# Pooled attention and a mixture of four attention experts: the order table's units divided at each change of engine, and the table arranged anew

## The chip, the cores and the metric

The kernel runs on one core of a Trainium2 chip. The metric is the device time of one execution in microseconds (us), median of the runs shown; less is better.

## What is computed

Eight batches, each with 8 heads, 576 rows and head size 64. First an attention whose keys and values are averaged in groups of 8 rows (72 pooled rows), then four causal attention experts over the joined heads (512 wide), of which the two with the highest gate logits are added per row:

```python
k_p = k.reshape(B, H, Sp, pool, D).mean(axis=3)      # pool = 8
v_p = v.reshape(B, H, Sp, pool, D).mean(axis=3)
attn = softmax(q @ k_p.T / sqrt(D))                  # 576 x 72 for each head
x = join_heads(attn @ v_p)                           # (B, 576, 512)
logits = x @ w_gate                                  # 4 experts
w = softmax of the two largest logits, 0 for the others
for e in range(4):
    a = softmax(causal((x @ wq[e]) @ (x @ wk[e]).T / sqrt(Hd)))
    out += w[..., e] * (a @ (x @ wv[e]) @ wo[e])
```

## The kernel before

The work of a batch is cut into **units**, small functions that each issue a few instructions on several engines. Rows 0 to 511 of a batch are its main part; the last 64 rows of two batches are taken together as one tail block of 128 rows (units of the odd batch). The units, with their lines in the kernel before:

- Loads (SyncE's DMA queue, SP): `lq`, `lk`, `lv` (main rows, 1 MB each; for batch 0 in two halves `lqa`, `lqb` and so on), `lqt`, `lkt`, `lvt` (the tails), `W:lq`, `W:lk`, `W:lv`, `W:lo` (weights; `W:lv` brings the small gate weights too).
- Preparation: `ks`, `vs` add neighbouring rows of k and v, `qc` casts q to bf16, `kt`, `vt`, `qt` cast the tails. From batch 1 on they run on GpSimd (POOL); for batch 0 they are spread over VectorE (DVE), ScalarE (ACT) and POOL.
- First attention: `kp` and `vp` pool k and v by matmuls; `q0` to `q3` transpose q; `s0` to `s3` make scores (matmuls that use 64 rows of the array) and their exponentials on ACT; `a0` to `a3` multiply by v and scale on DVE; `x0` to `x3` transpose the result.
- Experts: `v0`, `v2` make values and gate logits, `p0` to `p3` the projections (evacuated by ACT), `g1` to `g6` the gates (DVE, POOL, ACT and POOL, DVE, POOL), `c00`, `c01`, `c10`, `c11`, `c2` the causal scores (64-row matmuls, exponentials on ACT, masks on POOL), `o0`, `o1` the product with the values and its scaling on DVE, `t0`, `t1` transposes, and `w`, `y`, `z` units the product with `wo`, its evacuation by ACT or DVE and the store.
- Tail block: `qx`, `sx`, `ax`, `xx`, `pt`, `vx`, `h0`, `h1`, `hd`, `ox`, `tx`, `w4` in the same sense.

`in_order` keeps every instruction in the program's order on its own engine, so a program order is also each engine's queue. That order is written out by hand as the table `ORDER` of 501 unit names at the top; the last lines of the kernel run through it and call each unit once. A unit issues all its instructions at its place. If unit A stands ahead of unit B, then A's instructions are ahead of B's on PE, on DVE, on ACT, on POOL and on SP alike. For example `scores` of part A (unit `s`) issues two matmuls and the exponential together:

```python
            ps = ps2.tile([128, 2, MAIN], FP32, name="sA_ps", tag="ps2")
            ...
            et = etp.tile([SP, 2, MAIN], BF16, name="etA", tag="etA")
            act.activation(out=et[:], in_=ps[0:SP, :, :], func=EXP, scale=ATT_EXP_SCALE)
```

Matmul results go to two pools of PSUM buffers: `ps1` (2 buffers of one bank: `kp`, `vp`, `q`, `x`, `p`, `t`, `w`, `y` and the tail block's `qx`, `xx`, `pt`, `vx`, `ox`, `tx`, `w4`) and `ps2` (3 buffers of two banks: `s`, `a`, `v`, `c`, `o`, `z`, `sx`, `ax`, `h`, `hd`). A PE group waits until the engine that evacuates the buffer's previous content is through. Raw inputs have two buffers each, the tail of q one, output tiles four (`ofin`). All DMAs are issued by SP, in the table's order, and a store that waits for its copy holds back the loads behind it.

Of the kernel before, what the change touches and what calls it, by code (L numbers as in the profile page):

```python
# [53 lines left out]
def kernel(  # L54
# [126 lines left out]
    units = {}  # L181
# [49 lines left out]
    pairs = {}  # L231

    def part_a(b: int):
# [55 lines left out]
        def pool_k(p0, p1):  # L289
            ps = ps1.tile([128, NHP, SP], FP32, name="kpT_ps", tag="ps1")  # L290
            for hp in range(p0, p1):
# [9 lines left out]
                )  # L301
            dve.tensor_copy(out=kp[:, p0:p1, 0:SP], in_=ps[:, p0:p1, :])

        def pool_v():
# [5 lines left out]
            for half in range(2):  # L310
# [3 lines left out]
                )  # L314
            dve.tensor_copy(
# [3 lines left out]
        def q_t(hp):  # L319
# [3 lines left out]
            for r in range(NR):  # L323
# [3 lines left out]
                )  # L327
            dve.tensor_copy(
# [3 lines left out]
        def scores(hp):  # L332
            ps = ps2.tile([128, 2, MAIN], FP32, name="sA_ps", tag="ps2")
            for hh in range(2):
# [4 lines left out]
                )  # L339
            et = etp.tile([SP, 2, MAIN], BF16, name="etA", tag="etA")  # L340
# [3 lines left out]
        def av(hp):  # L344
# [4 lines left out]
            for hh in range(2):  # L349
                h = 2 * hp + hh  # L350
                for c in range(NTC):
# [4 lines left out]
                    )  # L356
            view = ps[:, :, 0 : NTC * (D + 1)].rearrange("p e (c d) -> p e c d", c=NTC)
# [11 lines left out]
        def x_t(fc):  # L369
            ps = ps1.tile([128, MAIN], BF16, name="xT_ps", tag="ps1")  # L370
            for c in range(NTC):
# [3 lines left out]
                )  # L375
            dve.tensor_copy(out=xT[:, fc, :], in_=ps[:])
# [32 lines left out]
    def part_p(b: int):  # L409
# [5 lines left out]
        def proj(j):  # L415
            ps = ps1.tile([128, MAIN], FP32, name="p_ps", tag="ps1")
            for fc in range(NFC):
# [3 lines left out]
                )  # L421
            act.copy(out=qk[:, j, :], in_=ps[:])
# [6 lines left out]
        def values(c0):  # L429
            L = logits()  # L430
            ps = ps2.tile([128, 2, 512], FP32, name="v_ps", tag="ps2")
            for cl in range(2):
                c = c0 + cl
                for fc in range(NFC):
# [3 lines left out]
                    )  # L438
            dve.tensor_copy(out=L[:, c0 : c0 + 2, :], in_=ps[:, :, E * HD : NVG])
# [84 lines left out]
    def part_s(b: int):  # L524
# [19 lines left out]
        def scores(ep, i):  # L544
            if ep not in st["et"]:
# [311 lines left out]
```

## Time and profile before

| | us |
|---|---|
| runs | 180.79, 181.35, 184.5 |
| median | 181.35 |
| span of the profiled execution (its own time) | 180.5 |
| PE busy | 157.6 |
| DVE busy | 131.6 |
| ACT busy | 121.4 |
| POOL busy | 105.0 |

The profile page and the trace belong to one execution, whose time is its span from the first to the last instruction. PE is TensorE, PEld its weight loads. A PE row's end is modelled: a matmul's record lasts longer than the time until the next may start, so the start-to-start time of two groups tells more than their durations. In a timeline row stand the start, the duration, the engine, the operation, output and inputs, the shape, the count, and in brackets the idle time before it with what ended it. Because every operation goes through one helper, all rows bear the helper's line L100, and groups are known by their tiles.

### The profile page before, as it was taken

To read this page: it belongs to the slowest core of one execution; us is meant where nothing else is said; L and a number is where in the kernel's file an instruction comes from. 1 tells how busy PE (TensorE), PEld (TensorE's weight loads), DVE (VectorE), ACT (ScalarE), POOL (GpSimd) and SP (SyncE) were. 2 spreads that over 40 slices of the span, in tenths; PEclk is the share of its full clock that TensorE was granted. 3 is DMA by queue.
4 is the path that set the end of the run, shared out by engine and by line. 5 is a ranking of instruction groups with operands and counts; after the bars stand their busy time and mean duration, and the time that the engine had idled before them with its cause. 6 is when DMAs were issued, how large, how long until landed. Compare 5 with 4: busy or idle time off the path is not lost.

```text
span 180.5 us, 5221 instructions
## 1 busy us (share of the span) xinstructions
PE 157.6 (87%) x2080; PEld 100.5 (56%) x2080; DVE 131.6 (73%) x363; ACT 121.4 (67%) x165; POOL 105.0 (58%) x212
## 2 busy tenths in 40 slices
PE   0046977799999999999999999999999999999970
PEld 0022465357766756765675667666666674665530
DVE  0166786589799787898877886977687877787850
ACT  2022600778497976887898688888788887778821
POOL 8953357437989879578988577726301253453200
PEclk9999999999999999999999999999999999999997
DMA  4999999999999999999999994325130333152964
GB/s 141 311 300 183 328 347 202 232 310 329 182 349 317 329 232 318 292 266 313 272 334 302 367 349 142 91 60 189 47 117 3 100 136 122 58 165 78 337 236 123
DMA packets 50200, 40.19 MB, mean 223 GB/s; under 512 B 20736, under 2 KB 45312, under 8 KB 50176
## 3 DMA queue, kind: packets, MB, share of 16 engines
q1 hardware_dynamic: 50176, 39.86, 79.6%
q8 instruction: 16, 0.26, 0.7%
q14 instruction: 8, 0.07, 0.1%
HBM read 30.42 MB, written 9.44 MB: 221 GB/s over the span
## 4 chain that ended last, share of the span: by engine, by line
PE 75%; SPq 13%; DMA 5%; DVE 2%; ACT 1%; issue 1%; POOL 1%; DVEq 0%; ACTq 0%; POOLq 0%
PE p_ps L100 15%; SPq L100 13%; PE y_ps L100 8%; PE v_ps L100 7%; PE sB_ps L100 6%; PE oB_ps L100 5%; DMA qtail<-in_q_dram 5%; PE xT_ps L100 4%; PE sA_ps L100 4%; PE oA_ps L100 4%; PE qT_ps L100 4%; PE oBt_ps L100 3%; PE oT_ps L100 2%; PE vp_ps L100 2%; PE pt_ps L100 2%; PE kpT_ps L100 2%
## 5 line engine op out<-in xcount | busy, mean ns | idle before, releaser
L100 ACT ACTIVATE etA<-sA_ps 72x1024 bf16<-72x1024 f32 x32 | 32.0, 1018 | 19.6 <-PE sA_ps L100 19.4
L100 ACT ACTIVATE etB<-sB_ps 128x1024 bf16<-128x1024 f32 x32 | 31.7, 1026 | 2.4 <-PE sB_ps L100 2.1
L100 PE MATMUL p_ps<-xT,wqk 128*128 128x512 bf16 x128 | 32.3, 379 | 0.0
L100 POOL TENSOR_SCALAR_AFFINE_SELECT etB<-etB 128x256 bf16<-128x256 bf16 x48 | 18.7, 407 | 14.9 <-ACT etB L100 12.4
L100 ACT CAST qk<-p_ps 128x512 bf16<-128x512 f32 x32 | 18.7, 584 | 12.3 <-PE p_ps L100 12.0
L100 DVE TENSOR_TENSOR x_tm<-oA_ps,rzA 128x512 bf16<-128x512 f32 x32 | 22.1, 692 | 1.1
L100 POOL TENSOR_TENSOR vsum<-vraw 128x512 bf16<-128x512 f32 (+1 forms) x16 | 19.0, 1210 | 3.9 <-DMA vraw<-in_v_dram 3.4
L100 PEld LDWEIGHTS <-wqk 128*128 128x128 bf16 x192 | 14.6, 97 | 10.4 <-issue 0.5
L100 POOL TENSOR_TENSOR ksum<-kraw 128x512 bf16<-128x512 f32 x14 | 17.4, 1266 | 3.4 <-DMA kraw<-in_k_dram 3.4
L100 PE MATMUL y_ps<-wo_t,oT 128*128 128x512 bf16 x64 | 18.2, 379 | 0.1
L100 PE MATMUL v_ps<-wvg,xT 128*128 128x260 bf16 x128 | 17.4, 281 | 0.1
L100 POOL CAST qbf<-qraw 128x2048 bf16<-128x2048 f32 x7 | 13.2, 1891 | 7.0 <-DMA qraw<-in_q_dram 7.0
L100 DVE COPY qT<-qT_ps 128x512 bf16<-128x512 bf16 x32 | 13.2, 419 | 4.4 <-PE qT_ps L100 3.9
L100 DVE COPY xT<-xT_ps 128x512 bf16<-128x512 bf16 x32 | 13.0, 419 | 2.9 <-PE xT_ps L100 2.6
L100 PE MATMUL qT_ps<-ident,qbf 128*128 128x128 bf16 x128 | 13.5, 235 | 1.5 <-DVE kp L100 0.7
L100 ACT COPY ofin<-y_ps 128x512 f32<-128x512 f32 x20 | 11.5, 586 | 4.8 <-ACT etB L100 1.9
L100 PE MATMUL sA_ps<-qT,kp 64*128 64x512 bf16 x64 | 12.8, 412 | 1.6 <-DVE kp L100 0.9
L100 PE MATMUL sB_ps<-qk 64*128 64x256 bf16 (+3 forms) x128 | 13.9, 300 | 0.2 <-ACT etB L100 0.2
L100 PEld LDWEIGHTS <-etA 72*128 72x128 bf16 x256 | 11.5, 101 | 4.2 <-ACT etA L100 0.7
L100 PE MATMUL oA_ps<-vp,etA 72*128 72x65 bf16 x256 | 13.6, 200 | 0.0
L100 PEld LDWEIGHTS <-xT 128*128 128x128 bf16 x128 | 12.1, 100 | 2.4 <-DVE xT L100 0.4
L100 PE MATMUL xT_ps<-perm,x_tm 128*128 128x128 bf16 x128 | 12.6, 231 | 0.8 <-DVE x_tm L100 0.7
(119 smaller groups left out, 324.0 us busy)
## 6 DMA issues: line engine op xcount, KB each, us to landing
qraw<-in_q_dram SPq DMA_DIRECT2D x7, 1024.0 KB, 9.2
kraw<-in_k_dram SPq DMA_DIRECT2D x7, 1024.0 KB, 8.3
vraw<-in_v_dram SPq DMA_DIRECT2D x7, 1024.0 KB, 10.4
out_dram<-ofin SPq DMA_DIRECT2D x28, 256.0 KB, 2.3
kraw<-in_k_dram SPq DMA_DIRECT2D x2, 512.0 KB, 4.8
ktail<-in_k_dram SPq DMA_DIRECT2D x16, 64.0 KB, 6.9
qraw<-in_q_dram SPq DMA_DIRECT2D x2, 512.0 KB, 7.3
vtail<-in_v_dram SPq DMA_DIRECT2D x16, 64.0 KB, 7.1
```

The source lines that it names most:

```text
L100: return tc.keep_in_program_order(fn(*args, **kwargs))
```

## The change

Each unit becomes a generator: where its work passes from one engine to another, a `yield` stands, and the table names the unit once for each part. The 501 names become 920 entries. The parts of a unit keep their order, and each engine's queue can now have an order of its own. The table is arranged anew over all engines; buffers, tiles and instructions stay. The tail buffer of q is made by whichever of the two batches loads first.

```diff
 ORDER = """
-0:lka 0:lkt 0:lkb 0:lqb 0:qcb1 0:lqa 0:lvt 0:ksb 0:qcb0 0:kt 0:lvb 0:qca0 0:kpb 0:lva W:lv 0:ksa
-1:lq 0:q3 0:qca1 0:vt 0:q0 0:q1 0:vsa 1:lkt 0:s3 1:lk 1:lv 0:kpa 0:lqt 0:vsb 0:vp 0:s0 1:qc 0:q2
-W:cv 0:s1 0:a0 0:s2 0:a3 0:a1 0:a2 0:x1 0:x3 1:q0 0:x2 1:lvt 0:x0 W:lq 1:q2 1:ks 0:v2 1:lqt 0:v0
-1:kt 1:q3 1:kp W:lk 0:g1 1:vs 2:lq 1:s2 1:s3 2:lkt 1:q1 W:c2 1:s1 0:g2 0:g3 1:vt 1:vp 2:lk 1:qt
-2:lv 0:g4 2:lqt 0:p2 W:c0 1:qx 1:a3 1:s0 2:qc W:c1 W:c3 0:p0 1:sx 1:a1 1:a2 3:lkt 0:p1 0:p3 2:kt
...
-7:c01 6:t1 5:y0 7:h0 5:y1 6:y1 7:o1 6:w2 6:w0 7:o0 5:w3 7:hd 7:h1 7:t1 7:t0 6:y3 7:z2 7:ox 7:z0
-7:tx 7:w4
+0:lkb 0:lqa 0:lka 0:ksb 0:lvt 0:lkt 0:ksa 0:lqb 0:lva 0:qca0 0:qcb1 0:kt 0:qcb0 0:q3 0:q3 0:qca1
+0:kpb 0:kpa 0:vsa 0:lvb 1:lq 0:kpb 0:q0 0:vt 0:q0 0:kpa 0:q1 0:q1 1:lk 0:s3 0:s1 0:s1 1:qc 0:q2
+0:vsb 0:s0 0:q2 0:s0 1:ks 0:vp 0:vp 0:a0 1:q1 0:a0 1:q0 0:s3 1:q1 1:lkt 0:lqt 0:s2 1:q0 0:x0 0:x0
+1:kt 0:a3 0:a3 1:q3 0:a1 1:q3 0:s2 1:q2 0:a1 0:a2 1:q2 1:lvt 1:lv 1:kp 1:vt 0:x3 1:kp 0:a2 1:s2 1:s0
+W:lv 0:x3 1:s2 1:lqt 0:x2 0:x1 1:s1 0:x1 0:x2 1:s3 1:vs 1:s1 W:cv 1:vp 0:v0 1:qt W:lq 1:s3 1:qx 1:vp
+1:s0 1:a1 1:qx 1:sx 1:a1 0:v2 0:v0 1:sx W:lk W:c0 1:a0 1:a3 W:c2 0:v2 1:a0 2:lq 0:g1 W:c3 0:g2 W:c1
+0:p0 0:p0 1:a2 0:p2 2:lvt 1:ax 1:ax 0:p3 1:a3 0:p2 0:p3 0:p1 0:g3 1:x1 1:a2 1:x1 0:c10 0:c11 0:p1
+1:xx 0:g4 0:c01 2:lkt 1:xx 1:x3 1:x0 1:x3 1:x0 0:c11 0:c2 1:x2 2:lk 0:c01 0:c00 1:x2 0:c2 2:qc 2:q1
+2:lv 2:q1 1:pt 1:vx 1:vx 1:pt 2:vt 2:kt 1:v2 0:c2 0:c11 2:q0 3:lk 1:p2 2:ks 0:c10 3:lkt 0:c00 1:p2
...
+5:y2 6:w2 7:o1 6:w2 6:w0 7:o0 6:w0 5:w3 7:t1 5:y0 6:y1 7:hd 5:w3 6:w0 7:h1 7:hd 7:hd 5:w3 7:h1 7:o0
+6:w2 7:t1 7:t0 6:y3 7:t0 7:z2 6:y3 7:ox 7:z2 7:z0 7:ox 7:tx 6:y3 7:tx 7:z0 7:w4 7:w4 7:w4
 """
...
-                if b % 2 == 0:
+                if b // 2 not in pairs:
...
         def scores(ep, i):
+            ps = piece([(ep, 0, 0)] if i == 0 else [(ep, 1, 0), (ep, 3, 384)])
+            yield
             if ep not in st["et"]:
                 st["et"][ep] = etbp.tile([128, 2, 1024], BF16, name="etB", tag="etB", bufs=3)
             et = st["et"][ep]
-            ps = piece([(ep, 0, 0)] if i == 0 else [(ep, 1, 0), (ep, 3, 384)])
             exps(et[:, :, i * 512 : i * 512 + 512], ps[:])
+            yield
             for col in (0,) if i == 0 else (512, 896):
                 causal(et[:, :, col : col + 128], 2)
...
             y(ps[:], c)
+            yield
             t = ofp.tile([128, DM], FP32, name="ofin", tag="ofin")
             copy(out=t[:], in_=ps[:])
+            yield
             store(out[b, c * 128 : c * 128 + 128, :], t[:])
...
+    parts = {}
     for name in ORDER.split():
-        units[name]()
+        if name not in parts:
+            parts[name] = units[name]() or iter(())
+        next(parts[name], None)
+    assert all(next(part, parts) is parts for part in parts.values())
```

The same single `yield` is put between the matmuls and the evacuation of `kp`, `vp`, `q`, `s`, `a`, `x`, `p`, `v`, `o`, `t` and of the tail block's units.

More of the change, by code (lines that the diff above doesn't have):

```diff
@@ new lines @@
+3:qx 1:c2 3:qc 3:lvt 1:c00 2:a2 2:x0 2:a3 1:c2 3:qx 1:c11 2:a3 3:kp 2:x2 1:h1 1:h0 4:lq 1:c11 3:kp
+2:x2 1:h1 2:x3 1:c10 3:q2 1:c00 2:x3 1:c2 3:q3 3:q3 1:c10 3:q2 3:vs 3:vt 4:lk 2:v2 4:lkt 3:q1 3:q1
+5:lq 1:g4 2:v2 2:v0 2:v0 4:lvt 0:t0 2:p1 3:s1 1:h0 2:p1 3:s3 3:sx 3:vp 3:s1 0:t0 2:g1 2:p0 3:sx 1:g5
+3:vp 4:qc 3:a1 1:g6 3:q0 1:c11 1:hd 3:s3 3:q0 3:ax 4:ks 1:c01 4:q2 2:p0 2:p2 3:a1 4:lv 4:q2 4:q1
+1:c01 4:kt 3:ax 1:c10 4:q1 3:a3 2:g2 2:p2 3:s2 3:s0 4:q0 1:ox 3:a3 W:lo 4:q0 3:xx 1:c01 5:lqt 2:c01
@@ new lines @@
+1:ox 3:s0 2:c00 3:s2 3:a2 3:xx 4:kp 3:pt 2:c01 4:kp 5:qc 2:c00 3:pt 3:x1 3:a2 5:lkt 3:x1 4:lqt 3:a0
+3:a0 1:o0 4:q3 2:p3 4:s2 4:s0 4:q3 1:o0 2:p3 4:vs 4:s2 6:lkt 3:x2 3:x0 1:o1 4:vt 5:kt 2:g3 3:x2 5:lk
+3:x0 3:x3 5:qt 6:kt 5:q2 2:c01 4:s1 4:s0 3:x3 5:q2 1:o1 3:p1 4:s1 1:t0 3:p1 1:t0 W:co 2:c2 2:c10
+4:s3 2:g4 1:t1 2:c2 4:vp 5:lvt 1:t1 4:vp 3:v0 4:s3 6:lvt 2:c10 5:q1 5:lv 4:a0 3:p3 4:a1 5:q1 4:a0
+3:p3 3:v0 0:w1 7:lkt 4:a2 4:a2 3:p2 6:lq 0:w1 2:c2 4:a1 2:c11 2:c00 3:h0 5:q3 5:q3 3:p2 2:c11 3:vx
@@ new lines @@
+3:hd 4:p3 4:v2 3:h1 2:t1 0:w0 5:xx 5:a3 5:a1 6:lqt 2:t1 5:a3 5:pt 6:vs 3:h1 6:q0 5:pt 3:c01 3:c00
+5:a1 1:w3 6:ks 6:q0 6:vp 3:c00 6:q3 4:v0 0:w2 7:kt 6:vp 1:tx 3:c01 4:c01 6:q3 4:c2 1:tx 3:c10 5:x0
+4:v0 4:c2 5:x0 6:kp 7:lv 3:o1 6:kp 5:x3 4:c01 7:lvt 2:w0 7:qc 4:c00 5:x3 6:s1 7:qt 3:o1 2:w0 6:s1
+7:q2 3:ox 4:c00 7:q2 5:x1 5:x1 6:a1 3:ox 6:a1 6:s3 5:p2 6:s3 1:w4 5:hd 3:c00 6:s0 5:p2 6:q2 6:q2
+1:w4 7:ks 6:a3 3:c01 7:kp 7:q3 5:hd 6:s0 7:kp 6:s2 6:x1 6:a0 7:q3 1:w2 6:x1 6:s2 1:w2 5:p3 7:qx 6:a2
+6:a0 5:p3 3:o0 6:a3 1:w0 7:qx 1:w4 2:w2 1:w0 6:a2 4:c11 1:w2 4:g1 4:c2 2:w2 7:s2 5:vx 7:vs 4:g2 7:vt
@@ new lines @@
+3:y1 5:g4 7:s0 7:x3 7:ax 2:w3 3:w0 5:g5 6:v0 3:y1 7:ax 5:c11 3:w0 6:v0 5:c11 3:w3 3:w3 5:g6 5:hd
+4:t0 6:c2 3:w3 4:t0 5:c01 4:t1 6:c2 7:a0 3:w4 5:c2 4:t1 5:ox 3:y1 3:w4 7:a0 7:x0 5:c01 7:x0 6:c01
+6:c11 5:c00 5:ox 5:c00 7:p2 7:p0 6:g1 7:p2 5:tx 5:o1 5:c00 6:c11 6:c2 5:c01 5:tx 7:p0 6:g2 4:w2
+6:c01 7:v0 7:xx 5:o1 7:xx 5:o0 4:w2 3:w2 7:p3 3:w2 7:p3 5:o0 6:g3 6:c00 4:w2 6:c10 4:y0 6:c00 3:w4
+6:c11 7:v0 4:y0 7:vx 7:v2 6:c10 5:w4 5:w4 7:vx 5:t0 7:v2 7:c11 5:t0 3:w0 7:c10 6:c00 5:t1 6:c01
+6:c10 7:g1 5:t1 6:g4 6:g5 6:g6 7:c11 4:w3 6:o1 4:y1 4:w3 7:c10 4:y0 4:y1 3:w2 5:y1 6:o0 7:c10 7:g2
@@ L421, in proj @@
                 )
+            yield
             act.copy(out=qk[:, j, :], in_=ps[:])
@@ L666, in scores @@
                         )
+            yield
             act.activation(
@@ L741, in scores_main @@
                         )
+            yield
             act.activation(
@@ L765, in scores_tail @@
                 )
+            yield
             for e in range(2):
```

60 lines of the change are left out of this document (38 added, 22 removed).

## The prediction

> **What bounds the kernel now.** I read the page's busy times and slices first, then busy time by stretch, then PE's timeline from start to start, because a busy PE need not be a PE at its peak.
>
> ```profile
> span 180.5 us, 5221 instructions
> ...
> PE 157.6 (87%) x2080; PEld 100.5 (56%) x2080; DVE 131.6 (73%) x363; ACT 121.4 (67%) x165; POOL 105.0 (58%) x212
> ...
> PE   0046977799999999999999999999999999999970
> ```
> ```profile
> 18.00:30.00 12.00, 10.96 (x96) 7.32 (x95) 8.62 (x22) 3.06 (x3) 6.19 (x6) 1.00 1.16 303
> 30.00:50.00 20.00, 17.82 (x234) 11.38 (x231) 15.81 (x44) 13.25 (x17) 13.09 (x22) 1.00 1.16 261
> ...
> 70.00:90.00 20.00, 19.98 (x304) 13.28 (x302) 17.04 (x44) 16.27 (x21) 15.60 (x27) 1.00 1.13 292
> ...
> 150.00:165.00 15.00, 15.00 (x173) 8.90 (x171) 11.16 (x39) 11.78 (x19) 6.04 (x21) 1.00 0.32 109
> ...
> 172.00:176.00 4.00, 2.68 (x43) 1.41 (x39) 2.26 (x6) 1.17 (x2) 0.00 (x0) 1.00 0.70 265
> ```
>
> The first number after each stretch's length is PE's busy time. From about 36 us to 172 us PE never stops (19.98 of 20, 15.00 of 15), while DVE has 16 to 17 of 20 and ACT about 16. So three stages have three limits: a start in which loads and evacuations keep PE short of work (to about 36 us), a long middle that PE sets, and an end of some 8 us. Finer queues on DVE, ACT and POOL can pay in the start and the end. In the middle a change pays only if PE itself gets less to do.
>
> **What PE pays for in the middle.** The same group costs different times, by its neighbour:
>
> ```profile
> 102.42 0.38 PE L100 MATMUL qT_ps<-ident,qbf 128*128 128x128 bf16 x4
> 102.64 1.03 PE L100 MATMUL p_ps<-xT,wqk 128*128 128x512 bf16 x4
> ...
> 107.32 0.39 PE L100 MATMUL qT_ps<-ident,qbf 128*128 128x128 bf16 x4
> 107.64 0.61 PE L100 MATMUL sB_ps<-qk 64*128 64x512 bf16 x6
> 108.18 0.29 PE L100 MATMUL oTt_ps<-ident,o_st 128*128 128x128 bf16 x2
> 108.40 0.39 PE L100 MATMUL sB_ps<-qk 64*128 64x384 bf16 x4
> 108.72 0.40 PE L100 MATMUL xT_ps<-perm,x_tm 128*128 128x128 bf16 x4
> ```
>
> Four transposes take 0.22 us up to a 128-row group (102.42 to 102.64), but 0.32 us up to a score group that uses 64 rows (107.32 to 107.64): going in costs 0.10. One score unit up to a 128-row group takes 0.32 (108.40 to 108.72), two in a row 0.54 (107.64 to 108.18), so the unit that is followed by another takes 0.22: going out costs 0.10 as well. Each unbroken run of 64-row units thus costs PE 0.20 us, however long the run. [...]
>
> **The change, part by part.** The instructions are the same: 2080 matmuls, and the same work on DVE, ACT, POOL and in 112 DMA issues. What moves is their order, now free for each engine within what the data allow.
>
> *PE's order.* I counted the runs of 64-row units (s, sx, c, h, hd) in the order in which each table starts PE's parts: 88 units stand in 63 runs before and in 51 after. After batch 1's scores, where PE is the limit, it is 57 against 46: 11 x 0.20 = 2.2 us, taken as -2.1 since a few such changes fall into waits. Nothing covers this: PE is busy on both sides.
>
> *The loads at the start.* The new table puts the weights' load W:lv behind all large loads of batch 1, and orders batch 0 as kb, qa, ka, tails, qb, va, vb.
>
> ```profile
> 10.46 4.80 SPq L100 DMA_DIRECT2D wg_f<-in_moe_w_gate_dram  x1
> 15.31 0.51 SPq L100 DMA_DIRECT2D qraw<-in_q_dram  x1
> ...
> 25.10 4.09 SPq L100 DMA_DIRECT2D qtail<-in_q_dram  x1
> ```
> ```profile
> 15.56 1.59 POOL L100 TENSOR_TENSOR vsum<-vraw 128x256 bf16<-128x256 f32 x2 [2.43 <-DMA vraw<-in_v_dram]
> 21.15 1.89 POOL L100 CAST qbf<-qraw 128x2048 bf16<-128x2048 f32 x1 [4.00 <-DMA qraw<-in_q_dram]
> 24.94 2.49 POOL L100 TENSOR_TENSOR ksum<-kraw 128x512 bf16<-128x512 f32 x2 [1.91 <-DMA kraw<-in_k_dram]
> ...
> 28.53 2.48 POOL L100 TENSOR_TENSOR vsum<-vraw 128x512 bf16<-128x512 f32 x2 [0.76 <-DMA vraw<-in_v_dram]
> 31.57 0.22 POOL L100 TENSOR_TENSOR g_lm<-L,g_mx 128x16 f32<-128x16 f32 x1 [0.56 <-DVE g_lo L100]
> ...
> 34.28 1.13 POOL L100 CAST qtb<-qtail 128x512 bf16<-128x512 f32 x1 [2.15 <-DMA qtail<-in_q_dram]
> 35.38 0.21 POOL L100 TENSOR_TENSOR g_w<-g_ex,g_msk 128x16 f32<-128x16 f32 x1
> ...
> 39.46 1.89 POOL L100 CAST qbf<-qraw 128x2048 bf16<-128x2048 f32 x1 [3.00 <-DMA qraw<-in_q_dram]
> ...
> 44.20 2.49 POOL L100 TENSOR_TENSOR ksum<-kraw 128x512 bf16<-128x512 f32 x2
> ```
> ```profile
> 11.90 0.43 DVE L100 CAST qbf<-qraw 128x512 bf16<-128x512 f32 x1 [1.17 <-DMA qraw<-in_q_dram]
> ...
> 15.66 1.77 DVE L100 TENSOR_TENSOR vsum<-vraw 128x256 bf16<-128x256 f32 x2
> 18.56 0.69 DVE L100 CAST vp<-vp_ps 72x512 bf16<-72x512 f32 x1 [1.13 <-PE vp_ps L100]
> ...
> 19.98 0.68 DVE L100 CAST wvg<-wv_f 128x1024 bf16<-128x1024 f32 x1
> ...
> 37.08 0.75 DVE L100 CAST wqk<-wk_f 128x512 bf16<-128x512 f32 x2
> ```
> ```profile
> 20.18 0.62 PE L100 MATMUL oA_ps<-vp,etA 72*128 72x65 bf16 x8
> ...
> 27.13 2.60 PE L100 MATMUL v_ps<-wvg,xT 128*128 128x260 bf16 x16
> 29.57 0.39 PE L100 MATMUL qT_ps<-ident,qbf 128*128 128x128 bf16 x4
> ...
> 35.47 0.40 PE L100 MATMUL qTt_ps<-ident,qtb 128*128 128x128 bf16 x4 [0.72 <-POOL qtb L100]
> ...
> 40.15 0.39 PE L100 MATMUL xT_ps<-perm,x_tm 128*128 128x128 bf16 x4
> ```
> ```profile
> 44.06 0.89 PE v_ps L100 x8
> ```
>
> The first user of a load tells when it landed. Here 1 MB takes about 3.6 us (k to v, 24.94 to 28.53), so of the 5.6 us between v of batch 0 and q of batch 1 (15.56 to 21.15) about 2.0 belong to W:lv with its gate weights. Moved back, q lands near 19.1, k near 22.5, v with the two tails now ahead of it near 27.5, W:lv near 29.5, and batch 1's q tail at 30.2 to 32.0 instead of 34.2. The bytes ahead of W:lk are the same, so it still lands near 36.
>
> I followed the first groups by hand through the new orders with these durations. The first transposes (0:q3) now need the last of the q halves and start at 13.3; all small evacuations follow in a row, and the v sum of 1.77 us begins only after them, at 16.8 against 15.66. The scores' exponentials no longer stand behind vp, which before began 0:a0 at 20.18; now vp's copy begins it at about 20.5. DVE then has a0, q1, q0, x0, a3, q3, a1, q2, kp, a2, x3, x1, x2 without a pause, so 0:x is complete at 29.0 (before 27.1, when v starts), but batch 1's q, kp and all four scores are done by then too. W:cv is at 29.6, 1:vp at 30.2, 0:v0 at 30.6, 1:qx at 32.1 (before 35.47). The DVE queue, where qx stands ahead of a1, v0 and W:c0, waits there for the tail about 0.9 us. The casts of wk end at 38.9 (before 37.83), p3 and p1 follow, and x1 comes at 40.2 with nearly the same PE work done as at 40.15 before (15.9 against 15.8 us, counted in PE's fastest start-to-start times). So the start is worth 0. Its bounds: -0.9 if the tail lands at 30.2 and DVE does not pause, +1.4 if it lands at 32.0 and everything behind qx slides with it. I take the middle, since both landings are equally near the rows.
>
> *The gates of batch 0.* With W:lv, 0:v0 and 0:v2 move from 27 to 31 us and later, so 0:g1 ends near 38 on DVE, g2 follows on POOL, g3 now stands behind p3's copy on ACT (near 40), and POOL's queue has 2:qc behind 0:g4. Before, g4 ran at 35.38 and 2:qc waited for its own load at 39.46; now 2:qc starts near 41.2, and 2:ks, behind two causal masks, near 46.0 instead of 44.20. The pooled k is then ready near 48.6, where PE's new order asks for it at 48.0: +0.5. It is 0 if PE is as late itself, +2.0 if the whole shift of POOL (1.8) and a wait at 2:vp show.
>
> *The middle otherwise.* Covers become a little thinner: the shortest PE work between a score unit and the AV unit that needs its exponential is 1.3 us against 1.8, between vp and its first user 0.9 against 1.3. An exponential of 1.02 us, with some 0.2 until PE's last matmul is through (a transpose group's record lasts 0.38, the next group starts after 0.22), just fits; the vp copy of 0.69 lacks 0.1. Each such place costs about 0.1: +0.2. Bounds: the waits that PE now has between 40 and 165 us add up to 2.0 us by my sum of start-to-start times over their fastest; half of them could go (-1.0), half as much could come on top (+1.0).
>
> *The stores.* The stores of the 32 w and y units become entries of their own, so SP no longer holds a load back behind a store that waits for its copy. That frees loads which nothing waits for: DMA's share is 0.32 in 150:165, and PE does not stop in the middle for a load. It counts 0; the price if a store is late is a wait for one of four output buffers, 0.1 to 0.7 us once.
>
> *The end.* PE's last ten groups are the same but for the place of 7:t1, and what follows them too:
>
> ```profile
> 174.11 0.28 PE L100 MATMUL oTt_ps<-ident,o_st 128*128 128x128 bf16 x2 [0.20 <-DVE o_st L100]
> 175.51 0.61 PE L100 MATMUL yt_ps<-wo_t,oTt 128*128 128x512 bf16 x2 [1.12 <-DVE oTt L100]
> ```
>
> The 1.12 us wait for DVE's oTt copy, behind 7:z0's copy in both orders, stays: 0.
>
> Sum: 180.5 - 2.1 + 0 + 0.5 + 0.2 + 0 = 179.1 us of span. The runs shown stand 0.3 (lowest), 0.8 (median) and 4.0 us above the profiled span; I add 0.3: 179.4.
>
> **The rivals.** *B, faster: the start and the waits pay too.* For it: every wait of DVE for PE in the start is one that an order of its own can fill. Then the start gives -0.9, the waits -1.0, and POOL and the covers nothing: 180.5 - 2.1 - 0.9 - 1.0 + 0.3 = 176.8. Against it: DVE has no pause left in 21 to 29 us of my walk.
>
> *C, slower: POOL's queue behind the gates.* 2:qc behind 0:g4, g4 behind ACT's g3, g3 behind p3. If p3 comes at the late bound, 1.4 us on, 2:qc, 2:ks and 2:vs all slide by 1.8 + 1.4, and PE waits about 2 us at 2:kp and another 0.8 at 2:vp beyond the late start: 180.5 - 2.1 + 1.4 + 2.8 + 0.2 + 0.3 = 183.1. It decides once 2:ks starts later than about 47.5 us, for then the loss is over 2.1. Against it: POOL has 13 of 20 us in that stretch and catches up.
>
> [...]
>
> **How the numbers follow.** Forecast A (about 177.4 to 181.3 by its terms) has 0.50, B 0.28, C 0.17, D 0.05. The time is A's, 179.4. The range reaches into B and C: 175.6 (B with the end's wait gone as well) to 183.6. Two per cent, about what a measurement of this kernel can tell from no change, is 3.6 us: faster means under 177.7, slower over 185.0. B mostly and a little of A lie under 177.7: 0.30. Over 185.0 needs C with more behind it: 0.10. Within: 0.60.
>
> **What would show it.** Right: PE without waits from about 50 us on, some 11 fewer 0.10 us steps each way, x1 of batch 1 near 40 us, 2:qc near 41. Wrong: x1 before 39 or after 42, waits of PE on DVE or POOL in the middle that add up to over 2 us, or an end whose last wait is not the one for oTt.

## The result, and the profile after

| | runs | median | range |
|---|---|---|---|
| kernel before | 4 | 181.15 us | 180.79 to 184.5 |
| changed kernel | 4 | 187.78 us | 183.92 to 192.63 |

The ratio of the changed kernel to the kernel before is 1.0145, with an interval of 1.010 to 1.019. Ratios here compare undisturbed executions alone; the profiled execution of the changed kernel is one of the long ones (span 190.8 us), in which the granted clock fell twice, so part of its length is told apart from the rest below. The forecast was 179.4 us, between 175.6 and 183.6: too fast.

The page of the changed kernel, busy times and slices:

```profile
span 190.8 us, 5181 instructions
...
PE 155.5 (81%) x2054; PEld 101.7 (53%) x2080; DVE 137.2 (72%) x363; ACT 120.8 (63%) x165; POOL 103.5 (54%) x212
...
PE   0048767999978989799999997199699999999980
...
PEclk9999995599999999999999999979999999999997
```

PE has no more work than before (155.5 us with 26 records missing, 157.6 before), but the unbroken row of nines is gone: there is a hole of a whole slice near 120 us and smaller ones near 55, 78 and 135 us. DVE has become longer by 5.6 us at the same 363 instructions. The clock row has two half-rate places. By stretches (PE's busy time stands behind the length, the clock is the third number from the end):

```profile
28.00:38.00 10.00, 8.34 (x70) 5.53 (x70) 6.42 (x21) 1.85 (x2) 0.83 (x2) 0.50 1.06 241
...
118.00:124.00 6.00, 1.02 (x22) 0.93 (x19) 5.31 (x3) 1.02 (x2) 4.26 (x7) 0.94 0.00 0
```

What PE waited for in the changed kernel, behind the 11.3 us before the first cast of q (us in total, times, longest):

```profile
PE xT_ps L120 <- DVE qT L120: 5.7, 3, 5.0
PE p_ps L120 <- ACT ofin L120: 1.6, 1, 1.6
...
PE sA_ps L120 <- DVE o_sc L120: 1.2, 1, 1.2
```

The first and the last are late DVE results (o_st is another, with 1.5 us), in the stage in which PE had no wait over a few tenths before. The longest, in DVE's timeline and then in POOL's:

```profile
116.40 0.20 DVE L120 RECIPROCAL rzB<-oB_ps 128x8 f32<-128x8 f32 x1
116.70 5.58 DVE L120 TENSOR_TENSOR gt<-rzB,g_G 128x8 f32<-128x8 f32 x1
122.32 0.69 DVE L120 TENSOR_TENSOR o_sc<-oB_ps,gt 128x512 bf16<-128x512 f32 x1
```
```profile
115.88 2.50 POOL L120 TENSOR_TENSOR ksum<-kraw 128x512 bf16<-128x512 f32 x2
...
119.78 2.48 POOL L120 TENSOR_TENSOR vsum<-vraw 128x512 bf16<-128x512 f32 x2
```

A multiplication of 128 x 8 numbers, both inputs in SBUF, lasts 5.58 us. It ends at 122.28, when POOL's unbroken row of eight instructions ends (two additions, four masks, two additions; 122.26), and PE, which needs the transposes' copy behind it, stands still:

```profile
118.23 0.19 PE L120 MATMUL oBt_ps<-vat,etD 128*128 128x65 bf16 x1
123.40 0.58 PE L120 MATMUL xT_ps<-perm,x_tm 128*128 128x128 bf16 x4 [4.97 <-DVE qT L120]
```

The group of this instruction over the whole kernel (min/median/max in ns), before and after:

```profile
L100 DVE TENSOR_TENSOR gt<-rzB,g_G x20: 165/168/898, 49.2 to 173.4; 128x8 f32<-128x8 f32 x16, 128x4 f32<-128x4 f32 x4
```
```profile
L120 DVE TENSOR_TENSOR gt<-rzB,g_G x20: 165/168/5585, 51.1 to 184.5; 128x8 f32<-128x8 f32 x16, 128x4 f32<-128x4 f32 x4
```

The medians are equal and hide it. The trace has six shorter holds as well (gt of 1.33, 1.20, 1.66 and 0.63 us, g_hi of 1.42 and 1.07). The five over 1 us each end within 0.05 us of the end of a single POOL instruction, an addition or a cast of q, for example

```profile
67.02 1.42 DVE L120 TENSOR_TENSOR g_hi<-L 128x8 f32<-128x8 f32 x1
```
```profile
66.53 1.89 POOL L120 CAST qbf<-qraw 128x2048 bf16<-128x2048 f32 x1
```

The 0.63 us took in two masks, the 5.58 us the whole row. Summed over every DVE instruction, the time above the fastest of its group is 7.3 us before and 16.1 us after.

From this came three theories. **P**: a DVE instruction with two inputs in SBUF is kept out while POOL works back to back, by chance for one POOL instruction or for a whole row, and the new order puts such rows where PE depends on it. **S**: the late load `W:lv` makes PE wait at 30 us, and the clock falls behind it. **Q**: POOL's queue, the rival C of the prediction. A fourth came with the second profile: **O**, an output buffer that comes free too late (the wait for `ofin` above).

### The profile page after: what moved, and what is told of

Read it like the earlier page. It is cut to its first block, busy times and chain, and to the rows that moved or that the text cites. A ratio compares the mean times of both kernels' runs of the same rounds, so it can differ in the third digit from the quotient of the medians.

```text
span 190.8 us, 5181 instructions
## 1 busy us (share of the span) xinstructions
PE 155.5 (81%) x2054; PEld 101.7 (53%) x2080; DVE 137.2 (72%) x363; ACT 120.8 (63%) x165; POOL 103.5 (54%) x212
## 4 chain that ended last, share of the span: by engine, by line
PE 56%; DVE 19%; DMA 11%; SPq 6%; ACT 4%; issue 2%; ACTq 0%; DVEq 0%
PE p_ps L120 12%; PE v_ps L120 8%; SPq L120 6%; DVE gt L120 6%; DMA wv_f<-in_moe_wv_dram 5%; PE y_ps L120 5%; PE sB_ps L120 5%; PE oA_ps L120 3%; PE oB_ps L120 3%; DMA kraw<-in_k_dram 3%; PE xT_ps L120 3%; PE qT_ps L120 2%; DVE o_sc L120 2%; DMA out_dram<-ofin 2%; PE oT_ps L120 2%
## 5 line engine op out<-in xcount | busy, mean ns | idle before, releaser
L120 PE MATMUL qT_ps<-ident,qbf 128*128 128x128 bf16 x128 | 13.1, 231 | 11.8 <-DVE qbf L120 11.3
L120 PEld LDWEIGHTS <-wqk 128*128 128x128 bf16 x192 | 15.2, 99 | 13.3 <-issue 4.0
L120 PE MATMUL v_ps<-wvg,xT 128*128 128x260 bf16 x128 | 18.6, 292 | 1.4 <-DVE wvg L120 1.0
L120 PEld LDWEIGHTS <-qbf 128*128 128x128 bf16 x128 | 8.6, 102 | 15.1 <-DVE qbf L120 11.3
L120 PE MATMUL y_ps<-wo_t,oT 128*128 128x512 bf16 x53 | 16.0, 379 | 0.3 <-issue 0.2
L120 PE MATMUL oA_ps<-vp,etA 72*128 72x65 bf16 x256 | 13.7, 201 | 2.4 <-DVE vp L120 1.3
L120 PEld LDWEIGHTS <-xT 128*128 128x128 bf16 x128 | 12.6, 102 | 4.6 <-DVE wvg L120 1.5
L120 PEld LDWEIGHTS <-x_tm 128*128 128x128 bf16 x128 | 8.4, 98 | 10.6 <-issue 7.3
```

What stands on the lines that cost most here:

```text
L120: return tc.keep_in_program_order(fn(*args, **kwargs))
```

## The experiments

**The changed kernel again**, in a second measurement.

> The changed kernel itself, for a second trace of it. Theory P (the port): DVE's small multiply gt, whose two inputs both lie in SBUF, does not get through while POOL works without a pause; it should again take over 1 us in at least three of its twenty places, at the same units as in the first trace (0:o1, 0:o0, 3:o1, 1:ox), and PE's waits for o_sc and o_st should follow it. Theory S (the start): PE again waits about 2.6 us for W:cv near 27 us, and whether the granted clock then falls to half decides between a time near 184 and one near 191. Theory Q (the queue, rival C of the prediction): 2:qc stands behind 0:g4, and PE's waits lie at 2:kp and 2:vp instead.

Measured: ten executions of 179.49 to 183.3 us, median 182.34, beside 182.09 for the kernel before; ratio 0.9914 (0.9844 to 0.9985). So the same program took 179.5 to 192.6 us over these two measurements. Its profile has a span of 178.0 us, and no gt was kept out for long, where theory P expected at least three over 1 us:

```profile
L120 DVE TENSOR_TENSOR gt<-rzB,g_G x20: 166/168/477, 48.6 to 171.6; 128x8 f32<-128x8 f32 x16, 128x4 f32<-128x4 f32 x4
```

Two profiles of one program, 12.9 us apart: their PE queues are the same, so the distance can be read group by group, by the difference of the starts. It grows to 2.95 us by 38 us, in the half-rate stretch; to 6.2 us by 82 us, in steps at the shorter holds (gt of 1.33, 1.20 and 1.66 us, g_hi of 1.42); by 5.2 us at the gt above; and by 1.4 in the half-rate stretch of 3.4 us right behind that stop. So holds of DVE make 3.3 + 5.2 = 8.5 us of it, the slower clock 2.95 + 1.4 = 4.4. The execution of 191.5 us has the same mean granted clock as the profiled one (0.957); those of 184.07 and 183.92 have 0.981 and 0.996. None of the three was profiled, but the last can have lost hardly anything to the clock.

**gt from PSUM** in the changed kernel: the reciprocal is written back in PSUM, so that gt has one input there and one in SBUF.

```diff
-        rz = osp.tile(rz_shape, FP32, name="rzB", tag=f"rzB{kind}")
-        dve.reciprocal(out=rz[:], in_=z)
+        dve.reciprocal(out=z, in_=z)
...
-        dve.tensor_tensor(out=gt[:], in0=rz[:], in1=gate, op=MULT)
+        dve.tensor_tensor(out=gt[:], in0=z, in1=gate, op=MULT)
```

> The changed kernel with one edit: the reciprocal in scaled is written over its own place in PSUM, so gt reads one input from PSUM and one from SBUF. Theory P: no gt over 0.4 us, PE's waits for o_sc and o_st (9 us in the first trace of the changed kernel) fall under 1.5 us, and the time falls by 3 to 8 us against the changed kernel, to 176 to 181. Theory S alone: gt gets short, but the time stays within 1 us, since PE's lost time comes from the start. Theory Q: no change beyond 1 us.

Measured: 180.45 us (177.89 to 181.55), ratio 0.9836 (0.9711 to 0.9961). That is 1.9 us less than the 182.34 of the unchanged order in the same measurement, where 3 to 8 were expected, and the two intervals overlap. All twenty gt took 161 to 167 ns, but the gate's instructions, which still read two SBUF operands, were kept out:

```profile
L120 DVE TENSOR_TENSOR g_msk<-L,g_m x8: 174/180/1870, 35.8 to 157.8; 128x16 f32<-128x16 f32 x4, 128x20 f32<-128x20 f32 x4
...
L120 DVE TENSOR_TENSOR g_hi<-L x8: 156/158/1309, 35.2 to 157.1; 128x8 f32<-128x8 f32 x4, 128x10 f32<-128x10 f32 x4
```

**W:lv ahead of batch 1's loads**, one entry of the table moved ahead of `1:lq`.

```diff
-0:kpb 0:kpa 0:vsa 0:lvb 1:lq
+0:kpb 0:kpa 0:vsa 0:lvb W:lv 1:lq
...
-W:lv 0:x3 1:s2 1:lqt
+0:x3 1:s2 1:lqt
```

> The changed kernel with W:lv issued ahead of 1:lq again, as in the kernel before; nothing else moves. Theory S: PE no longer waits for W:cv near 27 us (under 0.5), the clock is not cut after the start, and the time falls by 1.5 to 5 us; batch 1's q, k and v land about 2 us later, which takes back up to 1.5. Theory P: gt stays as long as before and the time stays within 1.5 us of the changed kernel's. Theory Q: 0:g1 to 0:g4 do not move, since 0:v0 keeps its place in PE's and DVE's order: within 1 us.

Measured: 184.35 us (183.69 to 185.12), ratio 1.0127 (1.0062 to 1.0191): slower than before and than the unchanged order. SP's queue shows the price of that place:

```profile
8.42 5.06 SPq L130 DMA_DIRECT2D wg_f<-in_moe_w_gate_dram  x1
13.52 0.50 SPq L130 DMA_DIRECT2D qraw<-in_q_dram  x1
14.07 1.12 SPq L130 DMA_DIRECT2D kraw<-in_k_dram  x1
```

The small gate weights hold SP for 5.06 us, and PE waits 2.1 us for batch 1's qbf instead. The clock does not fall again behind the start in this profile, and the kernel is slower all the same. As a remedy S falls. The place is not all of the loss: the profile has holds too (gt of 1.33 and 1.68 us, g_msk of 1.72).

**Both edits.**

> Both edits. If P and S are two separate losses, their gains add: 174 to 179. If P alone holds, as with gt from PSUM alone, within 1 us. If S alone holds, as with the early W:lv alone, within 1 us.

Measured: 181.72 us (179.5 to 183.15), ratio 0.9955 (0.9911 to 0.9998): the gain of the one and the loss of the other. Beside gt from PSUM alone, the early W:lv costs 181.72 - 180.45 = 1.3 us. The 174 to 179 us that two separate losses would have given did not come.

**Port-free.** This is a name only: no run shows what VectorE and GpSimd contend for. gt as above; the gate's maxima and minima as reductions of one operand; its comparison as a subtraction on POOL and a comparison with zero on DVE.

```diff
-            dve.tensor_max(out=hi[:], in0=L[:, :, 0:2], in1=L[:, :, 2:4])
-            dve.tensor_tensor(out=lo[:, :, 0:2], in0=L[:, :, 0:2], in1=L[:, :, 2:4], op=MINOP)
...
+            pair = L[:].rearrange("p t (a b) -> p t b a", a=2)
+            dve.tensor_reduce(out=hi[:], in_=pair, axis=AX_X, op=MAXOP)
+            dve.tensor_reduce(out=lo[:, :, 0:2], in_=pair, axis=AX_X, op=MINOP)
...
+            pool.tensor_tensor(
+                out=g("g_msk", E)[:], in0=gs["L"][:],
+                in1=gs["m2"][:].to_broadcast([128, NT, E]), op=SUB,
+            )
...
+            dve.tensor_scalar(
+                out=gs["g_msk"][:], in0=gs["g_msk"][:], scalar1=0.0, scalar2=None, op0=ISGE
+            )
```

> The changed kernel without the VectorE instructions that read two operands from SBUF in the gate and in the scaling: the reciprocal is written in place in PSUM and gt reads it there, the four maxima and minima of the gate are reductions over one operand, and the gate's comparison is split into a subtraction on GpSimd (one instruction more per batch) and a comparison with zero on VectorE. Theory P (VectorE is kept out while GpSimd works back to back): g_hi, g_lo, g_mx, g_msk and gt stay within 0.3 us of their fastest everywhere, the PE waits of over 1 us in which an o_sc or o_st was late are gone, ratio to the kernel before 0.983 (0.975 to 0.990), and the times spread less than 2 us. Theory S (the late W:lv and the half-rate stretch behind it): the start is as it was, ratio 0.99, spread as before, about 4 us. Rival R (the stall is not the operands but the place in the program: any small VectorE instruction there is late): reductions and mixed forms are as late as the old ones, one of 1 us or more in the profile.

Measured: 179.86 us (178.16 to 180.77), ratio 0.9868 (0.9797 to 0.994). The waits for o_sc and o_st of over 1 us are gone; the spread is 2.6 us, where under 2 was expected. The ratio alone does not tell this from the unchanged order's 0.9914, since the intervals overlap. The excess of all DVE instructions over their fastest fell to 4.3 us; the rows of gt (here without the tail block's four) and of the comparison:

```profile
L120 DVE TENSOR_TENSOR gt<-oB_ps,g_G x16: 165/166/167, 48.5 to 167.1; 128x8 f32<-128x8 f32 x16
```
```profile
L120 DVE TENSOR_SCALAR g_msk<-g_msk x8: 164/166/564, 38.4 to 162.0; 128x16 f32<-128x16 f32 x4, 128x20 f32<-128x20 f32 x4
```

The comparison with zero, with one input in SBUF, is not out of the contest: it is held here for 0.56 us, and in two later profiles once for 1.64 and 1.65 us beside POOL's cast of q. So "port-free" is not quite what the version is.

**The same edit on the kernel before**, as a control.

> The same edit on the kernel before, as a control. Theory P: it had the same forms with 7.3 us of delay over their fastest in its profile, the longest 0.9 us, of which little reached PE: ratio 0.995 (0.988 to 1.000), a smaller gain than the changed kernel's 0.8 per cent against itself. If the edit is worth as much here as there (1 per cent or more), the changed order is not what made VectorE late, and it was a cost of both kernels.

Measured: 181.92 us (181.38 to 183.79), beside 182.78 (180.98 to 185.16) unedited; ratio 0.9989 (0.9951 to 1.0027). The old order had the same instructions and lost hardly anything by them. By this pair it is the new order that makes them late where PE depends on them. The pair also gives what the order is worth without the holds: 179.86 - 181.92 = -2.1 us.

**The store moved.** In the second profile of the changed kernel the copy of 2:w2 waits for an output buffer:

```profile
122.46 0.59 ACT L120 COPY ofin<-y_ps 128x512 f32<-128x512 f32 x1 [1.80 <-DMA out_dram<-ofin]
```

2:w0's copy is through at 110.8 us, but its store stands behind that of 1:w4, whose copy comes at 114.4. One entry moves:

```diff
-... 1:w4 5:hd 3:c00 6:s0 5:p2 6:q2 6:q2 1:w4 7:ks ... 5:p0 5:vx 2:w0 3:o0
+... 1:w4 5:hd 3:c00 6:s0 5:p2 6:q2 6:q2 1:w4 2:w0 7:ks ... 5:p0 5:vx 3:o0
```

> The changed kernel with one entry moved: the store of 2:w0 ahead of the store of 1:w4, so that 2:w2 finds a free output buffer. Theory O: ScalarE's wait of 1.8 us for a store (at 120.7 to 122.5 us in its second profile), and PE's of 1.75 to 2.0 us between 5:vx and 5:p0, is gone and the end comes about 1.6 us earlier: ratio 0.982 against 0.991 of the unchanged order. Rival: PE's wait there is taken over by the next late item (ScalarE's copies behind it) and less than 0.5 us is gained. Theory P says nothing of this wait and expects VectorE's long gt and gate instructions to be there still, at some place or other, one of 1 us or more in the profile.

Measured: 181.2 us (178.28 to 190.73), ratio 0.9892 (0.9835 to 0.9948). The wait for the buffer is gone from PE's list, but against the unchanged order's 0.9914 the ratio is lower by 0.002 only, not by the 0.009 that theory O expected: by the times alone, its rival came true. The holds are there (a gt of 1.67 us), and so is the spread, 12 us, of the unedited forms: on one chip, the port-free version spread over 2.6 us in six executions and this one over 12 in twelve. In the three long ones (186.9 to 190.7 us) the mean granted clock was 0.962 to 0.975, in the others 0.987 to 1.000, so the clock has a part in this spread. The profile of this version has the same six shorter holds as the first profile of the changed kernel, each with the same length within 0.02 us and 2.9 us earlier; the second profile has none of them. So they are not drawn anew at each place, and what decides the first is open.

**Both.**

> Both edits together: the changed kernel without VectorE instructions that read two operands from SBUF in gate and scaling, and the store of 2:w0 moved ahead of that of 1:w4. If the two losses are independent, the span is that of the port-free one less ScalarE's wait for the output buffer (1.7 us in its profile): 177.8 - 1.7 = 176.1, about 178.0 as a median, ratio to the kernel before 0.976 (0.970 to 0.982); PE's last matmul group near 171.3; no run over 181. If a wait behind it takes over, 179.5 and ratio 0.985. If long runs (over 184, as the store-order version alone had) come back, the operands were not what made them.

Measured: 178.18 us (177.51 to 178.98), ratio 0.9773 (0.973 to 0.9817). This beats both kernels: the interval lies below 1 and below that of the unchanged order (0.9844 to 0.9985). It is also the test of theory P by time: with the store moved in both, taking the contested forms out changes the ratio from 0.9892 to 0.9773, and the intervals do not touch. The store is worth 179.86 - 178.18 = 1.7 us here (two chips; by the ratios 0.9868 - 0.9773, 1.7 us too), as its wait said, though the intervals overlap a little; with the contested forms in, it was worth 0.4. All waits of PE between 36 and 172 us, one line each:

```profile
PE qT_ps L121 <- POOL qbf L121: 0.3, 1, 0.3
PE oTt_ps L121 <- DVE o_st L121: 0.2, 1, 0.2
PE oT_ps L121 <- DVE o_sc L121: 0.2, 1, 0.2
```

**W:lv halfway**, ahead of `1:lvt`, on top of this version.

```diff
-1:q2 1:lvt 1:lv 1:kp
+1:q2 W:lv 1:lvt 1:lv 1:kp
...
-W:lv 0:x3 1:s2 1:lqt
+0:x3 1:s2 1:lqt
```

> The same with the weights W:lv loaded between the two places tried so far: behind 1:lqt and ahead of 1:lvt. Theory S in its weak form: PE's wait for the cast of these weights (1.1 to 2.4 us, between 1:vp and 0:v0) goes or halves without delaying batch 1's query rows, so the time is 0.5 to 1.2 us less than without the move. [...]

Measured: 183.69 us (182.77 to 187.9), ratio 1.008 (1.0042 to 1.0118): 5.5 us lost, where theory S gave a gain of 0.5 to 1.2. In this kernel's SP queue:

```profile
16.71 3.87 SPq L121 DMA_DIRECT2D wg_f<-in_moe_w_gate_dram  x1
...
22.21 0.60 SPq L121 DMA_DIRECT2D vraw<-in_v_dram  x1
```

I had counted the bytes of W:lv, not the 3.87 us for which its gate weights hold the queue. The sums of batch 1's v begin at 29.81 instead of 26.08, PE stands from 25.9 to 31.1, and the granted clock is half from 27.4 to 41.0 (in the profiled execution, 185.6 us). Where the change puts W:lv is the best of the three places.

**The runs of 64-row units split again**, on top of the best version: sixteen neighbours in PE's order change places, for example

```diff
-2:p1 3:s1
+3:s1 2:p1
...
-7:p3 3:w2 7:p3 5:o0 6:g3 6:c00
+6:c00 7:p3 3:w2 7:p3 5:o0 6:g3
```

> The best version so far (port-free, store of 2:w0 moved) with the one thing undone that the prediction's sum rests on: sixteen neighbouring PE entries between 62 and 153 us change places, so that the 64-row units stand in 66 unbroken runs again instead of 51 (before: 63). The work is the same, and each of the swapped units had its input 0.3 us or more before it was reached. If an unbroken run costs PE 0.20 us, as the prediction priced it, 15 runs more cost 3.0 us, less what stands in waits now: span 180.0 (179.2 to 181.0), ratio to the kernel before 0.993 against 0.977 without the swaps, and the loss is spread over the stretch from 62 to 153 us, about 0.2 us at each swap. Rival: the runs cost nothing, since PE waits for its inputs in between anyway, and the middle's gain came from other places of the order: under 0.8 us more, ratio 0.981 or less. If a swap makes a late input, a wait of 0.5 us or more stands at it and is told apart from the spread loss.

Measured: 181.17 us (180.72 to 185.24), ratio 0.9955 (0.9914 to 0.9996): 3.0 us more than without the swaps, as priced (3.3 by the ratios, which compare within each chip; the intervals do not touch). The first pair, without the swap and with it:

```profile
62.48 0.38 PE L121 MATMUL oT_ps<-ident,o_sc 128*128 128x128 bf16 x4
62.70 1.03 PE L121 MATMUL p_ps<-xT,wqk 128*128 128x512 bf16 x4
63.66 0.60 PE L121 MATMUL sA_ps<-qT,kp 64*128 64x512 bf16 x4
64.10 0.40 PE L121 MATMUL sAt_ps<-qTt,kp 64*128 64x64 bf16 x16
64.43 0.61 PE L121 MATMUL vp_ps<-vsum,pm 128*128 128x512 bf16 x2
```
```profile
65.25 0.38 PE L121 MATMUL oT_ps<-ident,o_sc 128*128 128x128 bf16 x4
65.57 0.39 PE L121 MATMUL sA_ps<-qT,kp 64*128 64x512 bf16 x2
65.89 1.04 PE L121 MATMUL p_ps<-xT,wqk 128*128 128x512 bf16 x3
66.86 0.39 PE L121 MATMUL sA_ps<-qT,kp 64*128 64x512 bf16 x2
67.08 0.40 PE L121 MATMUL sAt_ps<-qTt,kp 64*128 64x64 bf16 x16
67.41 0.61 PE L121 MATMUL vp_ps<-vsum,pm 128*128 128x512 bf16 x2
```

The same work, from one transpose group to the pooling of v, takes 64.43 - 62.48 = 1.95 us with the scores in one run and 67.41 - 65.25 = 2.16 us with the run cut in two: 0.21. Over the whole stretch the distance of the two traces climbs in such steps from 2.8 us ahead of the first swap (it stems from the start and from one hold) to 6.4 us behind the last, at 7:vx: 3.6 us by 15 runs, where the times give 3.0. The profiled execution is one of two long ones (185.24 and 185.11 us, mean granted clock 0.977 and 0.978): the clock was at half from 31.7 to 38.5 us. So executions over 184 us came back without the contested forms of gate and scaling, and by the expectation for both edits these forms are then not all that makes an execution long.

**The forms by themselves.** Nothing of the computation is left; while POOL runs a row of the pooling's additions (or masks, or fills), DVE issues small instructions of one form, twice, behind the second addition:

```python
for i in range(n):
    work(t, i)                      # POOL: an addition, a mask or a fill
    if i == 1:
        dve.tensor_copy(out=keep[:], in_=t[:, 0:8])
        op(d[:])                    # DVE: the form
        op(d[:])
```

> The forms by themselves; it leaves the whole computation out and writes zeros. In nine stages VectorE runs one small instruction twice (128 x 8 floats) while GpSimd works through eight or four instructions back to back: the addition of the pooling, 128x512 from two SBUF operands (stages a8, a4), the causal mask (m8), a fill (f8). The VectorE forms: two SBUF operands, PSUM and SBUF, a reduction of one operand, a comparison with a scalar per partition, a copy. Theory P: the form with two SBUF operands takes 0.16 us free and several us here, until GpSimd's row of additions ends (about the time of the six that are left in a8, of the two left in a4), and the mixed form, the reduction and the copy stay under 0.4 us; masks and fills lock it out for less. Rival R: every form is late alike, or none is. If it is let in between two additions, it takes at most the time of one addition, and the 5.6 us in the profile had another cause.

DVE's forms beside a row of additions: two inputs from PSUM and SBUF (0.35 us for two), a cast, and a copy:

```profile
25.39 1.21 DVE L27 CAST k_a8mixed<-p_a8mixed 128x8 f32<-128x8 bf16 x1 [2.71 <-POOL p_a8mixed L27]
...
26.51 0.35 DVE L27 TENSOR_TENSOR d_a8mixed<-ps,gate 128x8 f32<-128x8 f32 x2
26.90 0.92 DVE L27 COPY l_a8mixed<-d_a8mixed 128x8 f32<-128x8 f32 x1
...
43.85 8.57 POOL L27 TENSOR_TENSOR p_a8scalar<-araw 128x512 bf16<-128x512 f32 x7
45.15 7.30 DVE L27 CAST k_a8scalar<-p_a8scalar 128x8 f32<-128x8 bf16 x1 [7.44 <-POOL p_a8scalar L27]
```

The form with one PSUM input (153 and 166 ns) and the reduction (150 and 163 ns) were never held here. The two-SBUF form was, and so were casts and copies from SBUF to SBUF, which I had expected to be free: usually until the current addition ends (1.2 us), once, with a cast, over six of them (7.30 us). Rival R, that every form is late, falls. The two-SBUF form itself was held here for 1.1 and 1.3 us beside additions, not for the several us expected, and by the expectation's last sentence the 5.58 us would then have another cause. The next experiment answers that.

**The moment of arrival**: the copy to `keep` becomes one to seven reductions of `t`, which shift the arrival by 0.07 us each, and the form with two SBUF inputs follows once.

> The hold by itself, at several moments of arrival; the computation is left out and zeros are written. Twenty rows of eight GpSimd instructions back to back (fourteen of additions, three of masks, three of fills); in each, behind the second one, VectorE runs one to seven small reductions and then one instruction of two SBUF operands, so that it arrives at different moments of an addition. The reductions are not held (0.16 us each). If VectorE is let in at the next boundary between two GpSimd instructions, its instruction always ends within one addition (at most 1.3 us, the later it arrives the shorter); if it must win a race at each boundary, some rows hold it for two or more additions, up to the end of the row (about 7 us), and the two repetitions of the same arrival differ. In the first microbenchmark one of nine first instructions was held over six additions and one over six fills, so two to five of the twenty held longer than one are expected.

Fourteen rows of additions, and one of the long holds:

```profile
L27 DVE TENSOR_TENSOR d_a<-small,gate x14: 724/1030/7154, 10.2 to 140.4; 128x8 f32<-128x8 f32 x14
```
```profile
28.55 8.57 POOL L27 TENSOR_TENSOR row<-araw 128x512 bf16<-128x512 f32 x7
...
29.84 0.30 DVE L27 TENSOR_REDUCE k_a<-row 128x1 f32<-128x8 bf16 x3 [7.45 <-POOL row L27]
30.05 7.08 DVE L27 TENSOR_TENSOR d_a<-small,gate 128x8 f32<-128x8 f32 x1
```

Ten of the fourteen were let in at the next boundary (0.72 to 1.13 us, shorter the later they came), four were held over all six additions that were left (6.88 to 7.15 us), none in between. In four of the seven pairs with the same arrival one row was held long and the other was not: 0.29 us into an addition, 7.08 us once and 1.00 the other time. Of three rows of masks one held it over six (2.06 us); fills, which read nothing, did not hold this form (0.16 us; in the first microbenchmark it took 2.71 us among fills, behind a cast that was held itself). So the moment of arrival, to 0.01 us, does not decide it: a form that was not let in at the first boundary waited for the row's end, all four times. That is the shape of the 5.58 us in the kernel, and with the clock behind that stop it is what the profiled long execution has and the one of 178.0 us has not. That it is the cause of every long execution is not shown.

## Why the prediction was wrong

The step that failed is "The middle otherwise": +0.2, between -1.0 and +1.0. It listed the covers of exponentials and of vp with DVE's median durations, and so took a DVE instruction's duration as its own. What took its place is the hold of two-SBUF instructions by POOL's instructions and rows: 8.5 of the 12.9 us between the profiled execution and the one of 178.0. The other 4.4 are the clock, which the sum left out; D, a slow spell of PE, had 0.05. The row with the warning (gt, 165/168/898) was in the trace of before. In the microbenchmarks the form with two SBUF inputs was held beside additions (1.1 and 1.3 us), and so were a cast and a copy from SBUF to SBUF (1.21 and 0.92 us in the rows above); the form with a PSUM input (153 and 166 ns) and the reduction (150 and 163 ns) were not. One POOL instruction lasts 1.26 us as an addition and 1.89 as a cast of q. The five holds of 1.07 to 1.66 us in the kernel are of that size, each ending with one POOL instruction; the 5.58 us is not, and the long ones in the microbenchmark were six instructions, 7.1 us.

The other steps:

- **PE's order, -2.1: right.** Each run of 64-row units was priced at 0.20 us from rows of before; the first pair of the split experiment shows 0.21 and the whole of it 3.0 us for fifteen. What in PE costs this, no run shows. Counted again in the tables, it is 56 against 46 behind batch 1's scores and not 57, ten runs or 2.0 us. Between 1:x1 (PE's transposes at 39.28 and 39.75 us) and 7:x1 (136.70 and 139.01) the best version gains 1.84 us on the port-free kernel before.
- **The start, 0 (-0.9 to +1.4): mis-sized.** The walk had q landing near 19.1, v near 27.5 and 1:x1 at 40.2. In the 178.0 us profile the casts and sums on POOL began earlier (q's at 16.80, v's at 25.03), and 1:x1 came at 38.31, -1.8 against before (38.15 to 38.31 in four profiles with this start). The prediction gave W:lv 2.0 us of the wait for q; q's cast came 4.35 us earlier (21.15 to 16.80), and the row of 4.80 us for the gate weights on SP, which the prediction shows, is nearer to that:

```profile
16.80 1.90 POOL L120 CAST qbf<-qraw 128x2048 bf16<-128x2048 f32 x1 [2.74 <-DMA qraw<-in_q_dram]
...
39.73 1.89 POOL L120 CAST qbf<-qraw 128x2048 bf16<-128x2048 f32 x1 [0.21 <-DMA qraw<-in_q_dram]
...
44.08 2.49 POOL L120 TENSOR_TENSOR ksum<-kraw 128x512 bf16<-128x512 f32 x2 [0.32 <-DMA kraw<-in_k_dram]
```

  In the long profile 1:x1 came at 41.23, with the clock at half from 27.7 to 38 us.
- **The gates and POOL's queue, +0.5, and rival C: wrong in size.** 2:ks starts at 44.08 us (forecast 46.0, before 44.20). C did not happen.
- **The stores, 0 with 0.1 to 0.7 if late: too small.** The wait for an output buffer came in every profile with this order of stores, 1.6 to 1.8 us of PE's time. I priced one short wait, but three buffers sit full behind stores that the table puts late.
- **The end, 0: a misreading.** I wrote that oTt's copy stands behind 7:z0's in both orders. In the new one it is ahead (172.62 against 172.82 us in the 178.0 us profile), and the last group follows the last transposes after 0.67 us instead of 1.40: -0.7.
- **D, with 0.05 in the line of chances,** was a slow spell of PE behind the start. In the long profile one came, with the granted clock at 0.50 from 27.7 to 38.0 us, and cost 2.95 us there; in the one with the runs split it came from 31.7 to 38.5 us, and 1:x1 only at 40.97; in the others with this start it was shorter or missing.

The clean sum (start -1.8, middle -1.8 with +1.7 for the store, end -0.7, together -2.6 against a measured 178.0 - 180.5 = -2.5) lies near the forecast span of 179.1, because errors cancelled; that is luck. From span to time the prediction added 0.3, from runs that were not the profiled one; in every execution that was measured both ways the time is 1.7 to 2.1 us above its own span (179.76 against 178.0). The time is wrong because what varies from run to run was not in it.

What stays open: why all four executions of the first measurement were longer than the ten of the second (only one was profiled, and the one of 183.92 us had hardly any slow clock), and what lets the clock fall between 25 and 32 us. At the end of the 4.97 us stop it falls as well (0.50 from 123.3 to 126.7 us), but the best version's profile, in which no wait of PE between 18 us and the fall at 25.6 us is over 0.8 us, has one too.

## What to carry to other kernels

When a table is rearranged over several engines, list the VectorE instructions with two SBUF operands and SBUF copies that PE depends on, and see what GpSimd runs beside them: a maximum far above the median of one group (gt: 5585 ns against 168) is the sign, and a PSUM operand (161 to 167 ns in all twenty gt) or a reduction (150 and 163 ns) took the instruction out of the contest here, while a comparison with one SBUF input did not (held once for 1.64 us). Price a store's or load's place by the time that it holds its queue and by the buffers that wait behind it, not by its bytes: here 8 KB of gate weights held SP for 3.87 us, and one late store cost PE 1.6 to 1.8 us. Look at the spread of the runs and not only at their median, and read the granted clock beside it: in this case holds and slow clock both made runs long.

## What the runs showed of the hardware

- A DVE instruction with two SBUF inputs that met a row of POOL additions was let in at the first boundary in 10 of 14 cases (0.72 to 1.13 us) and waited for the end of the whole row in 4 (6.88 to 7.15 us); in none of the 14 was it let in at a later boundary.
- The granted clock was at half for 10.2 us (from 27.7 us) and for 3.4 us (from 123.3) in the long profile of the changed kernel, for 3.4 us (from 25.3) in its profile of 178.0 us, for 6.8 us (from 25.6) in the best version's and for 13.7 us (from 27.4) in the one with W:lv halfway. In the best version's it fell although PE had been busy for 2.7 of the 4 us from 22 to 26.
- The load of the gate weights held SP for 3.87 us (W:lv halfway), 4.42 (changed kernel), 4.80 (before) and 5.06 (W:lv early), more than the 1 MB loads behind it (0.50 and 1.12 us with W:lv early).
